# Weight loads on a second queue and reordered statistics in the opening of a layernorm, local attention and gated MLP kernel

## The chip, the cores and the metric

The kernel runs on one core of a Trainium2 chip. The metric is the device time in microseconds (us) of one execution; lower is better. A profile of one execution has a "span" (first to last instruction), which is about 1.8 us shorter than the time. Times inside a profile count from the start of the span.

The program is static: Python code plans every instruction with a model of durations, and writes one instruction list for each engine. In the traces below each engine takes its list in order and waits on semaphores (in the changed kernel VectorE sat idle for 0.85 us in front of an instruction whose own inputs were ready).

## The reference

`x` has 2048 rows (tokens) of 640 numbers, all bfloat16.

```python
xn = layernorm(x)                        # per row, no weights
q, k, v = xn @ wqkv                      # 640 -> 3*640, 32 heads of 20
# sliding attention: each token sees 8 keys, at distances 0, 2, ..., 14
o = softmax(q.k * 20**-0.5) . v
out = x + o @ wo + ((xn @ w_gate) * (xn @ w_up)) @ w_down
```

Only the opening matters here: x is cut into 16 tiles of 128 tokens; each tile is loaded, normalised, transposed, and then multiplied with the Q and K weights.

## The kernel before

How a tile goes through the opening (`op` plans one instruction on one engine, `Task` hands it to the planner; `dve` is VectorE, `act` ScalarE, `pe` TensorE, `sp` the sync engine, which here only issues DMAs):

```python
def front(t):
    # ... cut: names of the tile's buffers
    def stats(i):      # VectorE: statistics of one half of the 640 columns
        op("dve", lambda e: e.bn_stats(o, a), ...)
    def aggr():  ...   # VectorE: mean and variance from both halves
    def sqrt():  ...   # ScalarE: standard deviation
    def recip(): ...   # VectorE: 1 / standard deviation
    def apply(): ...   # VectorE for t < 6, one instruction of 640 columns

    yield have("x", t)
    if t == 1:
        yield have("sd", 0)              # tile 1 may start once tile 0's sqrt is planned
    for i in range(2):
        if t == 2 and i == 1:
            yield have("xnt", 1)
        yield Task("dve", lambda: stats(i), r=[x], prio=-1 if t == 1 and i == 0 else p)
    yield Task("dve", aggr, ...)
    yield Task("act", sqrt, ...)
    yield Task("dve", recip, ...)
    yield Task("dve" if t < N_DVE_A else "act", apply, ...)
    # ... cut: 5 transposes on TensorE into PSUM, then the copy back to SBUF
    #     (tile 0: columns 0-383 by VectorE, the rest by ScalarE); mark("xnt", t)
```

How the opening loads are issued, all but the touch on the sync queue:

```python
    x_load(0)
    stores.append(dma(TCH[0:16], tch, ..., name="touch", eng="act"))   # 5 KB of the weights, result unused
    x_load(1)
    wqkv_load(0, 0, 3)       # Q weights, first 3 of 5 chunks, 480 KB
    wqkv_load(0, 3, NCH)     # Q weights, last 2 chunks, 320 KB
    x_load(2)
    wqkv_load(1, 0, 3)       # K weights, the same way
    wqkv_load(1, 3, NCH)
    x_load(3)
    K.t["act"] = 2.1         # the planner takes ScalarE to be free from 2.1 us
    warm(18)                 # 18 matmuls of zeros, result unused
```

An x tile is 160 KB. After tile 0's transposes three more warm-up matmuls follow. The planner's belief about a load is one formula: it starts 1.2 us after its issue or when the load before it is through, moves 280 KB per us, and lands 0.8 us later.

Of the kernel before, what the change touches and what calls it, by code (L numbers as in the profile page):

```python
# [6 lines left out]
ALU = mybir.AluOpType  # L7
# [3 lines left out]
D = 640  # L11
NCH = 5
# [9 lines left out]
TS = 128  # L22
# [27 lines left out]
class Sched:  # L50
# [74 lines left out]
                deps[q.idx] = q  # L125
        return deps

    def op(self, eng, fn, r=(), w=(), dma=False, name="", occ=None, lat=None, lock=False, nbytes=0, mode=0, group=None, extra=0.0, acc=0.0):
        X = _Op()
        X.eng, X.fn, X.name, X.dma, X.group = eng, fn, name, dma, group  # L130
        X.needs_tick, X.event, X.pre_know, X.idx = False, None, None, len(self.ops)
        X.nth = self.n_eng[eng]
        self.n_eng[eng] += 1
        rk = [k for a in r for k in self.keys(a)]
        wk = [k for a in w for k in self.keys(a)]
        deps = self.deps_of(eng, rk, wk)
        if occ is None and not dma:
            occ = 0.1
        inorder = eng in ("pe", "act", "dve")
        start = max([self.t[eng]] + [d.end for d in deps.values()])  # L140
        if lock:
            start = max(start, self.t_lock)
        if eng == "pe" and mode != self.pe_mode:
            start += 0.1
            self.pe_mode = mode
        if dma:
            self.t[eng] = start + (0.48 if occ is None else occ)
            if acc:
                self.t_acc = max(self.t_acc, start + 3.8) + acc
                X.end = self.t_acc  # L150
            else:
                self.t_data = max(self.t_data, start + 1.2) + nbytes / 280e3
                X.end = self.t_data + 0.8 + extra
        else:
            self.t[eng] = start + occ
            X.end = start + (occ if lat is None else lat)
        if lock:
            self.t_lock = start + occ
        last = {}
        keep = []  # L160
        for d in deps.values():
            if d.dma or d.eng == "pool":
                keep.append(d)
            else:
                b = last.get(d.eng)
                if b is None or b.idx < d.idx:
                    last[d.eng] = d
        X.deps = keep + list(last.values())
        for d in X.deps:
            if not d.dma:  # L170
                d.needs_tick = True
        for k in rk:
            st = self.state.get(k)
            if st is None:
                self.state[k] = [None, [X]]
            elif inorder and st[1] and st[1][-1].eng == eng and not st[1][-1].dma:
                st[1][-1] = X
            else:
                st[1].append(X)
        for k in wk:  # L180
            self.state[k] = [X, []]
        if dma:
            if group is None or group not in self.groups:
                sem = self.nc.alloc_semaphore(f"dma{self.n_dma}")
                self.n_dma += 1
                if group is not None:
                    self.groups[group] = [sem, []]
            if group is None:
                X.event = (sem, 16)
            else:  # L190
                g = self.groups[group]
                g[1].append(X)
                X.event = (g[0], 16)
        self.ops.append(X)
        return X
# [151 lines left out]
def build_kernel(nc, A_x, A_wqkv, A_wo, B_x, B_w_gate, B_w_up, B_w_down, out):  # L347
    K = Sched(nc)
    op = K.op
# [3 lines left out]
    def sb(name, shape, dtype=BF16, at=None):  # L353
        n = mybir.dt.size(dtype)
        for s in shape[1:]:
            n *= s
        n = (n + 63) // 64 * 64
        if at is None:
            at = place[0]
            place[0] += n  # L360
        assert at + n <= 229344, (name, at + n)
        return K.sbuf(name, shape, dtype, at)
# [10 lines left out]
    NXS = 12  # L373
    XST = sb("XST", [128, NXS, D], at=a_ot + NCH * JB * 2)
# [43 lines left out]
    XNS = sb("XNS", [128, NXN, D], at=a_xr)  # L418
# [3 lines left out]
    MV = sb("MV", [128, NT, 2], FP32)  # L422
    SD = sb("SD", [128, NT, 4], FP32)
    DUM = sb("DUM", [128, 16], FP32)
    TCH = sb("TCH", [128, NCH, 32])
    ZERO = sb("ZERO", [128, JB])
    EPSC = sb("EPSC", [128, 16], FP32)
    IDENT = sb("IDENT", [128, 128])
# [15 lines left out]
    def mark(*k):  # L444
        done.add(k)
# [4 lines left out]
    def have(*k):  # L450
        return lambda: k in done
# [4 lines left out]
    xhbm = A_x[0]  # L456
    ohbm = out[0]

    def dma(o, i, r=(), w=(), name="", eng="sp", group=None):
        n = mybir.dt.size(o.dtype)  # L460
        for s in o.shape:
            n *= s
        return op(eng, lambda e: e.dma_start(o, i), r=r, w=w, dma=True, name=name, nbytes=n, group=group)  # L463

    op("dve", lambda e: e.memset(ZERO[:], 0.0), w=[ZERO[:]], name="zero", occ=0.2)
    op("dve", lambda e: e.memset(EPSC[:], EPS), w=[EPSC[:]], name="epsc", occ=0.1)
# [3 lines left out]
       r=[IDENT[:]], w=[IDENT[:]], name="ident", occ=0.4)  # L470
# [3 lines left out]
       r=[G[:]], w=[G[:]], name="g1", occ=0.3)  # L474
    op("pool", lambda e: e.affine_select(G[:], G[:], pattern=[[-4, H]], compare_op=ALU.is_ge,
                                         fill=0.0, base=0, channel_multiplier=1),
       r=[G[:]], w=[G[:]], name="g2", occ=0.3)
    op("pool", lambda e: e.memset(KT[:, :, 0:PAD], 0.0), w=[KT[:, :, 0:PAD]], name="kpad", occ=0.3)

    def xslot(t):  # L480
        return t + 4 if t < 8 else t - 8

    def x_load(t, eng="sp"):
        dma(XST[:, xslot(t), :], xhbm[t * TS:(t + 1) * TS, :], w=[XST[:, xslot(t), :]], name=f"xld{t}", eng=eng)
        mark("x", t)

    wqkv_src = A_wqkv.rearrange("(c p) n -> p c n", p=128)

    def wqkv_load(g, lo=0, hi=NCH):
        dst = WQKV[:, WPOS[g], lo:hi, :]  # L490
        dma(dst, wqkv_src[:, lo:hi, g * D:(g + 1) * D], w=[dst], name=f"ld_wqkv{g}_{lo}")

    def loads():
        def t(f, *a):
            return Task("sp", lambda: f(*a), prio=0)

        for t_ in range(4, NXS):
            yield t(x_load, t_)
        yield t(wqkv_load, 2)
        for t_ in range(NXS, NT):  # L500
            yield have("apply", t_ - NXS)
            yield t(x_load, t_)

        def w(T, src):
            dma(T[:], src.rearrange("(c p) n -> p c n", p=128), w=[T[:]], name="ld_w")

        def pads():
            z = ZERO[:, 0:PAD].unsqueeze(1).to_broadcast([128, NCH, PAD])
            dma(vscr[:, 0:PAD].rearrange("(c p) s -> p c s", p=128), z, r=[ZERO[:, 0:PAD]], w=[("vscr", "pad")], name="vpad")

        yield have("xnt", NT - 1)
        yield t(w, WG, B_w_gate)
        yield t(pads)
        yield t(w, WU, B_w_up)
# [15 lines left out]
    def front(t):  # L530
        x, st = XST[:, xslot(t), :], STATS[:, t, 0:12]
        xs, mv = XNS[:, t % NXN, :], MV[:, t, 0:2]
        sd, rstd, nmr = SD[:, t, 0:1], SD[:, t, 1:2], SD[:, t, 2:3]
        p = 0.1 * t

        def stats(i):
            o, a = st[:, 6 * i:6 * i + 6], x[:, i * DHALF:(i + 1) * DHALF]
            op("dve", lambda e: e.bn_stats(o, a), r=[a], w=[("st", t, i)], name=f"bn{t}_{i}", occ=0.49)  # L538
# [8 lines left out]

        def recip():
            op("dve", lambda e: e.reciprocal(rstd, sd), r=[("sd", t)], w=[("rstd", t)], name=f"rstd{t}", occ=0.16)  # L549
            if t >= N_DVE_A:  # L550
                op("dve", lambda e: e.tensor_scalar(nmr, mv[:, 0:1], rstd, -1.0, op0=ALU.mult, op1=ALU.mult),
                   r=[("mv", t), ("rstd", t)], w=[("nmr", t)], name=f"nmr{t}", occ=0.13)

        def apply():
            if t < N_DVE_A:
                op("dve", lambda e: e.tensor_scalar(xs, x, mv[:, 0:1], rstd, op0=ALU.subtract, op1=ALU.mult),
                   r=[x, ("mv", t), ("rstd", t)], w=[xs], name=f"lnap{t}", occ=0.45)
            else:
                op("act", lambda e: e.activation(xs, x, ACT.Identity, bias=nmr, scale=rstd),
                   r=[x, ("nmr", t), ("rstd", t)], w=[xs], name=f"lnap{t}", occ=0.75)  # L560
            mark("apply", t)
# [2 lines left out]
        if t == 1:  # L564
            yield have("sd", 0)
        for i in range(2):
            if t == 2 and i == 1:
                yield have("xnt", 1)
            yield Task("dve", lambda: stats(i), r=[x], prio=-1 if t == 1 and i == 0 else p)
        yield Task("dve", aggr, r=[("st", t, 1)], prio=p)  # L570
        yield Task("act", sqrt, r=[("mv", t)], prio=p - 1)
# [1 line left out]
        if t >= NXN:  # L573
            yield have("xnt", t - NXN)
        yield Task("dve" if t < N_DVE_A else "act", apply, r=[("rstd", t), x], w=[xs], prio=p)
        o = XNT[:, :, t * TS:(t + 1) * TS]
        if t < N_PE_T:
# [624 lines left out]
    stores = []  # L1202
# [65 lines left out]
    N_DVE_A = 6  # L1268
# [9 lines left out]
    H_PRIO = 9  # L1278
    FIN_PRIO = 8

    x_load(0)
    tch = A_wqkv.rearrange("(c k p) n -> k c p n", k=16, c=NCH)[:, :, 0, 0:32]
    stores.append(dma(TCH[0:16], tch, w=[TCH[0:16]], name="touch", eng="act"))
    x_load(1)
    wqkv_load(0, 0, 3)
    wqkv_load(0, 3, NCH)
    x_load(2)
    wqkv_load(1, 0, 3)
    wqkv_load(1, 3, NCH)
    x_load(3)  # L1290
    K.t["act"] = 2.1
    warm(18)

    def misc():
# [67 lines left out]
```

## Time and profile before

The time before was 270.0 us (median of 3, 269.71 to 270.01).

| | before | read from |
|---|---|---|
| span | 268.9 us | the page |
| TensorE (PE) busy | 262.7 us, 98% (18 of the 1783 matmul records are missing) | the page |
| first projection starts | 7.30 us | PE timeline |
| last gap before PE runs through | ends at 9.64 us | PE timeline |

The chain that ended last, from the page (shares of the span by engine, then by line):

```profile
span 268.9 us, 4464 instructions
...
PE 94%; DMA 2%; DVE 2%; issue 1%; SPq 0%; DVEq 0%
```

Nearly all is TensorE; the 2% of DMA is one load. The same chain in order of time (start, length, what), around that load:

```profile
1.73 5.44 DMA WQKV<-in_A_wqkv_dram
7.17 0.14 issue
7.30 0.84 PE PS L640 x12
...
9.09 0.50 DVE XNT L604
9.60 0.05 issue
9.64 1.98 PE PS L640 x32
```

The first projection (L640) hung on the first Q weight load, issued at 1.73 and landed at 7.17. The PE timeline (start, length, engine, line, operation; in brackets the idle time before it and what ended it):

```profile
1.27 4.02 PE L624 MATMUL PS<-ZERO 128*128 128x256 bf16 x18 [1.27 <-DVE EPSC L466]
5.42 0.71 PE L585 MATMUL PS<-IDENT,XNS 128*128 128x128 bf16 x5
5.92 0.85 PE L624 MATMUL PS<-ZERO 128*128 128x256 bf16 x3
7.30 1.48 PE L640 MATMUL PS<-XNT,WQKV 128*128 128x128 bf16 x20 [0.53 <-DMA WQKV<-in_A_wqkv_dram]
8.61 0.44 PE L585 MATMUL PS<-IDENT,XNS 128*128 128x128 bf16 x5
9.64 1.98 PE L640 MATMUL PS<-XNT,WQKV 128*128 128x128 bf16 x32 [0.59 <-DVE XNT L604]
```

L624 are warm-ups, L585 transposes. PE is nearly without a hole from 1.27 to 6.77. VectorE in the same stretch:

```profile
3.22 0.89 DVE L538 BATCH_NORM_STATS2 STATS<-XST 128x6 f32<-128x320 bf16 x2 [1.98 <-DMA XST<-in_A_x_dram]
4.14 0.21 DVE L541 BATCH_NORM_AGGREGATE MV<-STATS 128x2 f32<-128x12 f32 x1
4.27 0.44 DVE L538 BATCH_NORM_STATS2 STATS<-XST 128x6 f32<-128x320 bf16 x1
4.71 0.16 DVE L549 RECIPROCAL SD<-SD 128x1 f32<-128x1 f32 x1
4.91 0.45 DVE L556 TENSOR_SCALAR XNS<-XST,MV,SD 128x640 bf16<-128x640 bf16 x1
```

The third line is already tile 1: its first half of statistics fills the time in which VectorE would wait for tile 0's square root.

### The profile page before, as it was taken

To read this page: it belongs to the slowest core of one execution; us is meant where nothing else is said; L and a number is where in the kernel's file an instruction comes from. 1 tells how busy PE (TensorE), PEld (TensorE's weight loads), DVE (VectorE), ACT (ScalarE), POOL (GpSimd) and SP (SyncE) were. 2 spreads that over 40 slices of the span, in tenths; PEclk is the share of its full clock that TensorE was granted. 3 is DMA by queue.
4 is the path that set the end of the run, shared out by engine and by line. 5 is a ranking of instruction groups with operands and counts; after the bars stand their busy time and mean duration, and the time that the engine had idled before them with its cause. 6 is when DMAs were issued, how large, how long until landed. Compare 5 with 4: busy or idle time off the path is not lost.

```text
span 268.9 us, 4464 instructions
## 1 busy us (share of the span) xinstructions
PE 262.7 (98%) x1765; PEld 152.8 (57%) x1783; DVE 222.9 (83%) x282; ACT 105.4 (39%) x188; POOL 130.3 (48%) x81
## 2 busy tenths in 40 slices
PE   7899999999999999999999999999999999999996
PEld 5796975444444444444444445765457654676775
DVE  4678899999999997379999899999999989992212
ACT  3369998556723232245344353024430342201000
POOL 1000000000004439900199999999999879985000
PEclk9999999999999999999999999999999999999999
DMA  6954479621414998087025953465534561022201
GB/s 206 367 188 74 98 105 339 247 97 56 142 39 113 234 244 177 0 268 151 2 52 140 240 118 79 132 176 138 152 79 130 148 195 42 27 73 61 87 28 49
DMA packets 40261, 35.58 MB, mean 132 GB/s; under 512 B 15408, under 2 KB 38448, under 8 KB 40240
## 3 DMA queue, kind: packets, MB, share of 16 engines
q1 hardware_dynamic: 39424, 33.15, 45.4%
q0 software_dynamic: 576, 2.10, 3.9%
q8 instruction: 14, 0.23, 0.4%
q10 hardware_dynamic: 240, 0.05, 0.1%
q14 instruction: 7, 0.06, 0.1%
HBM read 25.07 MB, written 5.26 MB: 113 GB/s over the span
## 4 chain that ended last, share of the span: by engine, by line
PE 94%; DMA 2%; DVE 2%; issue 1%; SPq 0%; DVEq 0%
PE PS L1149 36%; PE PS L1231 28%; PE PS L640 24%; PE PS L903 3%; DMA WQKV<-in_A_wqkv_dram 2%; PE PS L1098 2%; DVE HT L1158 1%; PE PS L585 0%; DVE RS L952 0%; DVE LOG L956 0%; SPq L463 0%; DVE XNT L604 0%; DVE SM L932 0%; DVE FOUT L1244 0%; DVEq L325 0%
## 5 line engine op out<-in xcount | busy, mean ns | idle before, releaser
L1056 POOL TENSOR_TENSOR SV<-PV 128x1024 bf16<-128x1024 f32 x40 | 93.5, 2366 | 24.7 <-DVE LOG L956 18.7
L1051 DVE TENSOR_TENSOR PV<-VX,PS 128x1024 f32<-128x1024 bf16 (+1 forms) x56 | 91.8, 1670 | 0.3 <-POOL SV L1056 0.3
L640 PE MATMUL PS<-XNT,WQKV 128*128 128x512 bf16 (+2 forms) x474 | 66.4, 299 | 1.6 <-DVE XNT L604 0.6
L1149 PE MATMUL PS<-XNT,WU 128*128 128x512 bf16 x239 | 59.6, 380 | 0.2
L1149 PE MATMUL PS<-XNT,WG 128*128 128x512 bf16 x229 | 57.3, 380 | 0.7 <-issue 0.3
L640 PEld LDWEIGHTS PS<-XNT,WQKV 128*128 128x128 bf16 x480 | 43.6, 113 | 23.8 <-DVE SD L549 1.0
L1149 PEld LDWEIGHTS PS<-XNT,WU 128*128 128x128 bf16 x240 | 23.3, 98 | 28.7 <-ACT XNT L645 0.8
L1149 PEld LDWEIGHTS PS<-XNT,WG 128*128 128x128 bf16 x240 | 23.2, 98 | 28.6 <-issue 0.8
L792 DVE TENSOR_TENSOR PRD<-QT,KT 128x2048 bf16<-128x2048 bf16 x32 | 36.8, 1217 | 0.0
L1244 DVE TENSOR_TENSOR FOUT<-PS,XR 128x320 bf16<-128x320 f32 (+1 forms) x33 | 15.7, 479 | 22.2 <-PE PS L1231 22.0
L1231 PE MATMUL PS<-WD,HT 128*128 128x320 bf16 x192 | 28.7, 300 | 0.0
L645 ACT ACTIVATE HT<-PS 128x512 bf16<-128x512 f32 x24 | 14.3, 596 | 34.0 <-PE PS L1149 34.0
L1231 PE MATMUL PS<-WO,OT 128*128 128x320 bf16 (+1 forms) x165 | 27.0, 296 | 0.0
L863 POOL TENSOR_TENSOR PRF<-PRF,PRF 128x1024 f32<-128x1024 f32 x4 | 9.4, 2352 | 33.1 <-DVE PRF L837 33.0
L1107 ACT ACTIVATE OT<-PS 128x512 bf16<-128x512 f32 x20 | 10.5, 600 | 34.4 <-PE PS L1098 34.4
L922 POOL MEMSET LOG<- 32x6 bf16 (+6 forms) x7 | 0.4, 95 | 48.4 <-ACT LOG L914 48.4
L1158 DVE TENSOR_TENSOR HT<-HT,PS 128x512 bf16<-128x512 bf16 x24 | 16.3, 680 | 8.7 <-PE PS L1149 7.0
L1231 PEld LDWEIGHTS PS<-WD,HT 128*128 128x128 bf16 x192 | 18.8, 98 | 7.6
L1231 PEld LDWEIGHTS PS<-WO,OT 128*128 128x128 bf16 x165 | 15.7, 98 | 6.6 <-issue 0.8
L837 DVE TENSOR_TENSOR PRF<-PS,KT 128x1024 f32<-128x1024 f32 x16 | 19.0, 1216 | 0.4 <-DMA PRF<-PRF 0.4
L538 DVE BATCH_NORM_STATS2 STATS<-XST 128x6 f32<-128x320 bf16 x32 | 14.7, 471 | 3.0 <-DMA XST<-in_A_x_dram 3.0
L1231 PE MATMUL PS<-WD,XNT 128*128 128x320 bf16 (+1 forms) x108 | 14.6, 285 | 0.0
(58 smaller groups left out, 216.1 us busy)
## 6 DMA issues: line engine op xcount, KB each, us to landing
VX<-v_scratch SPq DMA_DIRECT2D x80, 130.0 KB, 2.9
XST<-in_A_x_dram SPq DMA_DIRECT2D x16, 160.0 KB, 6.2
v_scratch<-VST SPq DMA_DIRECT2D x4, 640.0 KB, 4.3
XR<-in_A_x_dram SPq DMA_DIRECT2D x16, 160.0 KB, 2.9
out_dram<-FOUT SPq DMA_DIRECT2D x15, 160.0 KB, 1.8
PRF<-PRF POOLq DMA_DIRECT2D x4, 512.0 KB, 8.6
WG<-in_B_w_gate_dram SPq DMA_DIRECT2D x1, 1920.0 KB, 8.6
WU<-in_B_w_up_dram SPq DMA_DIRECT2D x1, 1920.0 KB, 12.1
```

The lines of the kernel that those rows point to most:

```text
L538: op("dve", lambda e: e.bn_stats(o, a), r=[a], w=[("st", t, i)], name=f"bn{t}_{i}", occ=0.49)
L640: op("pe", (lambda o, l, x, c, first: lambda e: e.matmul(o, l, x, start=first, stop=(c == NCH - 1)))(o, l, x, c, first), r=[l, x], w=[o], ...
L645: X = op("act", (lambda o, i: lambda e: e.activation(o, i, ACT.Copy))(o, i), r=[i], w=[o], name=name, occ=0.12 + n * 0.9e-3)
L792: op("dve", lambda e: e.tensor_tensor(s[:], qb, kv, ALU.mult), r=[q, rk], w=[s[:]], name=f"prod{j}_{r}_{c}", occ=1.15, lock=True)
L837: X = op("dve", lambda e: e.tensor_tensor(o[:], qb, kv, ALU.mult), r=[q, rk], w=[o[:]], name=f"prow{j}_{r}_{c}_{q0}", occ=1.17)
L1051: op("dve", lambda e: e.tensor_tensor(p, vw, a, ALU.mult), r=[vv] + rk, w=[p], name=f"pv{u}_{x}_{r0}", occ=0.09 + 1.1 * nr)
L1056: X = op("pool", lambda e: e.tensor_tensor(o, p[:, :, 0, :], p[:, :, 1, :], ALU.add), r=[p[:]] + tokens(), w=[o], name=f"pva{u}_{x}", occ= ...
L1107: X = op("act", (lambda o, b: lambda e: e.activation(o, PS[:, b, :], ACT.Copy))(o, b), r=[PS[:, b, :]], w=[o], name=f"oev{u}", occ=0.58)
L1149: op("pe", (lambda l, x, c: lambda e: e.matmul(PS[:, b, :], l, x, start=(c == 0), stop=(c == NCH - 1)))(l, x, c), r=[l, x], w=[PS[:, b, :] ...
L1158: X = op("dve", lambda e: e.tensor_tensor(h, h, PS[:, hold[1], :], ALU.mult), r=[h, PS[:, hold[1], :]], w=[h], name=f"h{m}_{j}", occ=0.65)
L1231: op("pe", (lambda l, x, i: lambda e: e.matmul(dst, l, x, start=(i == 0), stop=(i == n - 1)))(l, x, i), r=[l, x], w=[PS[:, b, :]], name=f" ...
L1244: X = op("dve", lambda e: e.tensor_tensor(o, PS[:, b, 0:wid], xr, ALU.add), r=[PS[:, b, :], xr], w=[o], name=f"fin{t}_{nb}", occ=0.15 + wi ...
```

## The change

The intent: the weights should come sooner, so they are issued first thing on the scalar queue, which is idle, while the x tiles stay on the sync queue; x tile 3 waits until tile 0's reciprocal, so as not to compete. Tile 0 is applied in two parts, so that three transposes can start before the rest is applied. Half of tile 1's statistics and all of tile 2's go behind the copies that PE waits for. The planner is told a landing time for each load (`land=`) in place of its formula.

```diff
-    def op(self, ..., acc=0.0):
+    def op(self, ..., acc=0.0, land=None):
+            if land is not None:
+                X.end, self.t_data = land, max(land - 0.8, self.t_data - nbytes / 280e3)
     # x_load, wqkv_load and dma pass land and the queue on
     def x_load(t, ...):
+        r = [("rstd", 0)] if t == 3 else []          # x tile 3 after tile 0's reciprocal
     def apply():
-            if t < N_DVE_A:
+            if t == 0:
+                for a, b in ((0, 384), (384, D)):    # ... tensor_scalar of columns a to b
+            elif t < N_DVE_A:
     # in front(t):
-            if t == 2 and i == 1:
-                yield have("xnt", 1)
+            if t == 2 and i == 0:
+                yield have("apply", 1)
+            if t in (1, 2) and i == 1:
+                yield have("xnt", t - 1)
     # the opening loads:
-    x_load(0)
-    stores.append(dma(TCH[0:16], tch, w=[TCH[0:16]], name="touch", eng="act"))
-    x_load(1)
-    wqkv_load(0, 0, 3)
-    wqkv_load(0, 3, NCH)
-    x_load(2)
-    wqkv_load(1, 0, 3)
-    wqkv_load(1, 3, NCH)
-    x_load(3)
-    K.t["act"] = 2.1
+    x_load(0, land=3.2)
+    wqkv_load(0, 0, 3, "act", 5.4)
+    x_load(1, land=4.3)
+    wqkv_load(0, 3, NCH, "act", 6.7)
+    x_load(2, land=5.7)
+    wqkv_load(1, 0, 3, "act", 7.9)
+    wqkv_load(1, 3, NCH, "act", 8.9)
+    K.t["act"] = 4.1
     warm(18)
# ... cut: removal of the buffer TCH, argument lists, mark("rstd", t); loads() now starts
#     with x tile 3 and waits for tile 0's reciprocal
```

## The prediction

> **What bounds the kernel.** The chain of waits puts 94% of the 268.9 us span on the tensor engine (PE busy 98%, granted clock 1.00) and only 2% on a DMA: the Q weight load, issued at 1.73 us, ends 5.44 us later (7.17). The PE timeline shows the only real hole in its first 9.64 us: warm-up matmuls, five transposes (5.42), three more warm-ups (to 6.77), 0.5 us waiting for weights, 20 Q matmuls of tile 0 from 7.30 (1.48), transposes of tile 1 (8.61), then 0.59 idle until tile 1's copy ends. From 9.64 on PE runs almost gapless to 266. So up to 9.64 it has done only about 1.9 us of useful work: anything won can be won there alone, at most some 3 us.
>
> Why is the weight late? The DMA packets of the trace: one 1280-byte packet of that first weight load, started at 3.56, took 2.05 us; the other lanes had delivered by about 5.0. The following loads' completions inherit the roughly 2 us lag (x tile 2 lands at 8.47, the first K part at 9.8). The small touch load did not prevent it. Tile 1's chain adds its part: DVE waits for x tile 2 until 8.49, runs its first statistics there, and only then copies tile 1.
>
> **What the change does.** It removes the 5 KB touch, starts the Q and K weights at about 0.83, 1.25, 1.7, 2.1 on the scalar queue (0.43 us each) instead of 1.73, 2.2, 3.25, 3.7, and defers x tile 3 until tile 0's reciprocal (about 4.9). Bytes are unchanged. The Trainium skill, "DMA: Bandwidth & Descriptors", section "Issuing engines are not separate DMA queues", says that both queues use the same 16 engines and interleave, so only issue time is saved; I expect no more bandwidth, but the slow first weight packet about 1.4 us earlier. Costs: the 1.28 us activation table load moves to about 2.6 to 3.9, still before the first square root (4.38); x tiles 0 and 1 share the engines with weights, so they may land 0 to 0.5 us later (before: 3.2 and 3.6). Splitting tile 0's apply adds one DVE instruction (an estimate of 0.1 us from the 0.45 us whole) and lets three transposes start some 0.15 us earlier, but the 18 warm-ups end at 5.29 anyway. Moving half of tile 1's statistics (0.49 us) behind tile 0's copy frees DVE for that copy about 0.2 us earlier.
>
> **Expected times.** Q weights land near 5.4 and 6.7, K weights near 7.9 and 8.9. The first projection then hangs on tile 0's copy and the warm-ups: near 6.3 instead of 7.30. K matmuls of tile 0 fill the gap that waited for tile 1. The continuous stretch gains 1.0 + about 0.4 = 1.4 us, an estimate.
>
> **Does it survive?** From 9.64 to the end PE is the chain; DVE waits on that chain around 128 to 133 us cost PE nothing. GpSimd's last sum ends at 245.4 and PE takes it at 247.1: 1.6 us of slack, so 1.4 us passes even if that branch does not move. But the static order of all engines is computed again from new assumed times; that may shift the later order by about a microsecond either way.
>
> **Prediction: 268.6 us, range 267.4 to 269.9.** Faster by over 2%: 0.02; within 2%: 0.96; slower by over 2%: 0.02.
>
> **Right if** the first projection starts at 6.0 to 6.6, K matmuls precede tile 1's Q, the chain's DMA piece shrinks below 1%, and PE busy time is unchanged. **Wrong if** the slow packet also holds up x tile 0 (first statistics after 3.7), if a weight load still ends after 7, if the table load delays the first square root, or if the recomputed order starves PE later, after 100 us.

## The result, and the profile after

| | median | range | executions |
|---|---|---|---|
| before | 269.69 us | 269.48 to 270.01 | 6 |
| after | 271.55 us | 270.55 to 271.92 | 6 |

Ratio 1.0058, 95% interval 1.0038 to 1.0078: slower by 0.6%. Within 2%, so of the predicted class, but outside the predicted range and of the wrong sign. A ratio here is the mean time of one kernel's fast executions over that of the other's of the same rounds, so it is not quite the ratio of the medians. Executions in which one die ran at a lower clock are left out of the means. The spread, 1.37 us, is more than twice that of before, 0.53.

The page of after, the chain that ended last:

```profile
span 269.8 us, 4479 instructions
...
PE 97%; DMA 2%; DVE 0%; SPq 0%; issue 0%
```

Its opening in order of time:

```profile
1.28 4.14 DMA XST<-in_A_x_dram
5.42 0.02 issue
5.44 0.49 DVE STATS L541
...
6.03 0.39 DVE XNS L562
...
7.82 2.13 PE PS L651 x20
```

The load on the chain is now an *x tile*, not a weight. VectorE and PE (line numbers moved by the change: L541 statistics, L552 reciprocal, L562 apply in parts, L596 transposes, L635 warm-ups, L651 projections):

```profile
3.46 0.89 DVE L541 BATCH_NORM_STATS2 STATS<-XST 128x6 f32<-128x320 bf16 x2 [2.22 <-DMA XST<-in_A_x_dram]
4.38 0.21 DVE L544 BATCH_NORM_AGGREGATE MV<-STATS 128x2 f32<-128x12 f32 x1
5.44 0.49 DVE L541 BATCH_NORM_STATS2 STATS<-XST 128x6 f32<-128x320 bf16 x1 [0.85 <-DMA XST<-in_A_x_dram]
5.85 0.14 DVE L552 RECIPROCAL SD<-SD 128x1 f32<-128x1 f32 x1
6.03 0.64 DVE L562 TENSOR_SCALAR XNS<-XST,MV,SD 128x384 bf16<-128x384 bf16 x2
```

```profile
1.27 4.02 PE L635 MATMUL PS<-ZERO 128*128 128x256 bf16 x18 [1.27 <-DVE EPSC L467]
6.47 0.72 PE L596 MATMUL PS<-IDENT,XNS 128*128 128x128 bf16 x5 [1.18 <-DVE XNS L562]
6.97 0.85 PE L635 MATMUL PS<-ZERO 128*128 128x256 bf16 x3
7.61 2.34 PE L651 MATMUL PS<-XNT,WQKV 128*128 128x128 bf16 x20
9.75 0.74 PE L596 MATMUL PS<-IDENT,XNS 128*128 128x128 bf16 x5
10.28 2.68 PE L651 MATMUL PS<-XNT,WQKV 128*128 128x128 bf16 x40
```

Two things went wrong. First, VectorE waited 0.85 us for x tile 1, with tile 0's reciprocal standing behind that wait; its square root had ended at 4.9. Tile 0 was applied at 6.03 instead of 4.91, although its own data came only 0.24 us later. Second, the same 20 matmuls of the first projection took 2.34 us instead of 1.48. The groups of PE instructions from 7 to 10.2 us (count, then busy time and mean ns of one), before:

```profile
L640 PE MATMUL PS<-XNT,WQKV 128*128 128x128 bf16 x30 | 2.2, 221 | 1.1 <-DVE XNT L604 0.6 <-DMA WQKV<-in_A_wqkv_dram 0.5
```

and after:

```profile
L651 PE MATMUL PS<-XNT,WQKV 128*128 128x128 bf16 x20 | 2.3, 314 | 0.0
```

314 ns for 221: the tensor clock was not yet released. In the instruction records these matmuls start 107 ns apart after and 56 ns apart before. The trace's own clock record begins at full clock at 6.77 us before, at 10.43 us after. (The page's row of the clock is no help: it shows 9, the top tenth, in its first slice too, as the record begins only with the release.)

Where the rest of the time went is quickly said: nowhere. On the chain in order of time the first sums of the logits start at 47.91 before and 48.85 after, and the last instruction at 266.56 and 267.50: the same 0.94 us at both. The loss is complete before 48 us, and almost all of it arises before 11.

The landings (last of a load's 16 completions, read from the trace; "believed" is what the planner of the changed kernel was told):

```
                 x0     x1     x2     Q first  Q rest  K first  K rest   (us)
before          3.20   3.61   8.46    7.17     8.03    9.80    10.71
after           3.44   5.42   6.96    4.97     6.39    8.09     8.99
believed        3.2    4.3    5.7     5.4      6.7     7.9      8.9
```

The weights did what was wanted of them. x tile 1, issued at 1.28 us in both kernels, paid: 1.8 us later. The packets of the trace show how it was served:

```
after: KB moved in quarter microseconds, by queue
from     2.50 2.75 3.00 3.25 3.50 3.75 4.00 4.25 4.50 4.75
sync       23   19    6    0    0    0   25   78   49    9
scalar      8   41   79   89   92   86   66   20   46   82
```

What the sync queue moved up to 3.25 us was x tile 0. The first packet of x tile 1 started at 4.04 us, when some 400 KB of the 480 KB weight load, issued 0.45 us before it, had been started. By 4.5 us the two queues were moving side by side again.

### The profile page after: what moved, and what is told of

The parts are those of the page before. It is cut to its first block, busy times and chain, and to the rows that moved or that the text cites. A ratio compares the mean times of both kernels' runs of the same rounds, so it can differ in the third digit from the quotient of the medians.

```text
span 269.8 us, 4479 instructions
## 1 busy us (share of the span) xinstructions
PE 265.0 (98%) x1783; PEld 154.2 (57%) x1783; DVE 223.1 (83%) x283; ACT 105.5 (39%) x188; POOL 130.3 (48%) x81
## 4 chain that ended last, share of the span: by engine, by line
PE 97%; DMA 2%; DVE 0%; SPq 0%; issue 0%
PE PS L1160 39%; PE PS L1242 28%; PE PS L651 25%; PE PS L914 3%; PE PS L1109 2%; DMA XST<-in_A_x_dram 2%; PE PS L596 1%; PE PS L635 0%; DVE STATS L541 0%; SPq L464 0%; DVE XNS L562 0%; DVE FOUT L1255 0%; DVE SD L552 0%
## 5 line engine op out<-in xcount | busy, mean ns | idle before, releaser
L651 PE MATMUL PS<-XNT,WQKV 128*128 128x512 bf16 (+2 forms) x480 | 68.0, 303 | 0.0
L1160 PE MATMUL PS<-XNT,WG 128*128 128x512 bf16 x240 | 59.7, 379 | 0.0
L651 PEld LDWEIGHTS PS<-XNT,WQKV 128*128 128x128 bf16 x480 | 44.8, 115 | 22.2 <-ACT LOG L925 0.8
L541 DVE BATCH_NORM_STATS2 STATS<-XST 128x6 f32<-128x320 bf16 x32 | 14.8, 473 | 3.1 <-DMA XST<-in_A_x_dram 3.1
```

The costliest lines, as they stand in the source:

```text
L541: op("dve", lambda e: e.bn_stats(o, a), r=[a], w=[("st", t, i)], name=f"bn{t}_{i}", occ=0.49)
L651: op("pe", (lambda o, l, x, c, first: lambda e: e.matmul(o, l, x, start=first, stop=(c == NCH - 1)))(o, l, x, c, first), r=[l, x], w=[o], ...
L1160: op("pe", (lambda l, x, c: lambda e: e.matmul(PS[:, b, :], l, x, start=(c == 0), stop=(c == NCH - 1)))(l, x, c), r=[l, x], w=[PS[:, b, :] ...
```

## The experiments

Three theories and their rival:

- **Theory 1**: x tile 1 is served behind the first Q weight load, and its statistics stand in front of tile 0's reciprocal on VectorE.
- **Theory 2**: the hole of 1.18 us in PE's warm-up moves the release of the clock to a later moment. (Every clock record that runs from the release to the end lasts a whole number of steps of 3.413 us: 259.41, 262.83 and 266.24 us are 76, 77 and 78 of them. Such a step is the "window" of the expectations.)
- **Theory 3**: the slow weight load in the first profile of before is not typical, so the baseline had less to win than was counted.
- **Rival**: the recomputed order, the split apply or the deferred x tile costs the time, later or by itself.

Four kernels went to a chip together; each was timed against the kernel before there. Where "program order unchanged" is said, the instruction lists of PE, VectorE and GpSimd were compared with those of the kernel it was made from, and differ in nothing but what the edit names.

### The changed kernel again

No edit.

> The changed kernel, unaltered, for a second look at what varies. Theory 1 (x tile 1 is served behind the whole first Q weight load, and its statistics stand in front of tile 0's reciprocal on VectorE): x tile 1 lands again near 5.4 us (5.2 to 5.6), reciprocal of tile 0 near 5.85. Theory 2 (the tensor clock is released one window later because PE idles from 5.3 to 6.5): release after 9 us in most executions, and the spread of the times, 270.5 to 272.0, is that release falling earlier or later. Rival (the late schedule is worse): the first 11 us look like those of before, and the loss appears after 20 us. Time 271.5, spread 1 us or more.

Five fast executions: 270.62, 270.72, 270.75, 271.65, 271.75; median of the fast ones 270.75, ratio 1.004 (1.0024 to 1.0056). The profiled one: clock 0.85, so its times prove little, but x tile 1 landed at 5.39 in it, as expected. Its clock record begins at 4.86 us, before PE's hole: the release can come early in the unaltered changed kernel, too. Together with the first six executions there are two groups and nothing between them: five with a span of 268.7 to 268.8 us, six with 269.7 to 270.1. Whether the clock was released after 9 us in most executions could not be checked here for want of a fast trace.

### Tile 0's applies in front of tile 1's statistics

```diff
         if t == 1:
-            yield have("sd", 0)
+            yield have("apply", 0)
```

This moves one VectorE instruction behind three others; PE's program order is unchanged.

> One VectorE instruction moved: the first half of tile 1's statistics goes behind tile 0's two applies. Theory 1: the wait for x tile 1 leaves tile 0's chain; reciprocal of tile 0 near 5.0 (was 5.85), transposes start near 5.55 (was 6.47), first projection 6.6 to 6.9 (was 7.61); that alone is worth about 0.8 us. Theory 2: PE's hole shrinks from 1.2 to about 0.3 us, the clock is released near 7, another 1.2 us. Both: 269.3 to 270.0. Theory 1 alone: 270.7. Rival (late schedule): 271.5, unchanged.

Measured: 269.95 us (269.89 to 269.99, 5 executions), before 269.96; ratio 0.9997 (0.9986 to 1.0009). VectorE and PE:

```profile
5.05 0.17 DVE L552 RECIPROCAL SD<-SD 128x1 f32<-128x1 f32 x1 [0.36 <-ACT SD L547]
5.26 0.64 DVE L562 TENSOR_SCALAR XNS<-XST,MV,SD 128x384 bf16<-128x384 bf16 x2
5.81 0.49 DVE L541 BATCH_NORM_STATS2 STATS<-XST 128x6 f32<-128x320 bf16 x1
```

```profile
5.69 0.71 PE L596 MATMUL PS<-IDENT,XNS 128*128 128x128 bf16 x5 [0.41 <-DVE XNS L562]
6.20 0.56 PE L635 MATMUL PS<-ZERO 128*128 128x256 bf16 x3
6.65 1.31 PE L651 MATMUL PS<-XNT,WQKV 128*128 128x128 bf16 x20
```

x tile 1 landed at 5.68, as late as in the changed kernel, but no longer held anything up. The first projection started 0.96 us earlier, the clock was released at 6.33, and the spread of 1.4 us shrank to 0.1. One instruction's place explains the whole loss. It also shows that the loss is not in the later order, which this kernel shares with the changed one. But the repaired change is *level* with before, not 1.4 us faster: this asked for theory 3.

### More warm-up matmuls

```diff
-    warm(18)
+    warm(24)
```

PE's and VectorE's order is otherwise unchanged; ScalarE copies two of the Q and K results out of PSUM in the other order.

> Six more warm-up matmuls (24 for 18), so that PE is busy until about 6.6 instead of 5.3; the wait for x tile 1 stays. Theory 2: the clock is released near 7 instead of 10.4, the 20 Q matmuls of tile 0 take about 1.2 us instead of 2.1, time 270.2 to 270.6 although the first projection still starts at 7.4 to 7.7. Theory 1 alone: no gain, 271.5. Rival (late schedule): 271.5.

Measured: 270.73 us (270.56 to 270.89), ratio 1.0026 (1.0014 to 1.0038), spans 268.7 to 268.9 in all five executions: the fast group of the changed kernel without the slow one. VectorE still waits for x tile 1, and PE still waits for VectorE, but it counts at full clock when it goes on:

```profile
6.76 0.54 PE L596 MATMUL PS<-IDENT,XNS 128*128 128x128 bf16 x5 [1.16 <-DVE XNS L562]
...
7.55 1.31 PE L651 MATMUL PS<-XNT,WQKV 128*128 128x128 bf16 x20
```

The clock was released at 4.45 us in this trace, so the later warm-ups ran at full clock and ended near 5.6, and PE's wait is as long as in the changed kernel, but harmless to the clock. In an execution with a later release, 24 warm-ups at the half-clock spacing of 0.213 us would last until 1.27 + 24 x 0.213 = 6.4 us (an estimate from the spacing in the changed kernel's trace), which closes the hole. This one trace would have released as early with 18 warm-ups; what counts is that none of the five executions is in the slow group, where 6 of 11 were. (Alone, that could be chance about 6 times in 100; the next experiment is the other half of the test.) So the two costs come apart: theory 2 is the distance between the groups, some 1.1 us in about half of the executions; theory 1's wait is what is left between this kernel and the repaired one, 268.7 against 268.0 us of span.

### Fewer warm-up matmuls

```diff
-    warm(18)
+    warm(12)
```

The dose in the other direction; nothing else moves.

> The changed kernel with 12 warm-up matmuls for 18: PE falls idle near 4.0 instead of 5.3, so its hole before the transposes grows from 1.2 to about 2.5 us; nothing else moves. Theory 2 (the hole decides at which window the tensor clock is released): no window that ends between about 5 and 9 is busy enough, so nearly every execution is a late one: release after 9 in the trace, times 271.4 to 272 with few or none near 270.6; median 271.6. If the hole does not decide: same two groups as the changed kernel, about half and half.

Measured: 272.23 us (271.55 to 272.55, 6 executions), ratio 1.0074 (1.0056 to 1.0091). No execution was in the fast group.

```profile
6.58 0.71 PE L596 MATMUL PS<-IDENT,XNS 128*128 128x128 bf16 x5 [2.57 <-DVE XNS L562]
7.09 0.85 PE L635 MATMUL PS<-ZERO 128*128 128x256 bf16 x3
7.73 2.34 PE L651 MATMUL PS<-XNT,WQKV 128*128 128x128 bf16 x20
```

The clock was released at 12.09 us in the trace. The median was 0.6 us worse than expected, as the release can come even later than in the changed kernel's trace. With 12, 18 and 24 warm-ups 6 of 6, 6 of 11 and 0 of 5 executions had a span of 269.7 us or more. With 18 warm-ups and a hole of only 0.41 or 0.43 us (the two repaired kernels) it was 0 of 11. So PE's hole decides.

The Trainium skill, "TensorE: Matmul & The Clock Gate", section "What's actually happening", says why: a monitor watches free-running windows of about 3.4 us, and the clock goes from half to full after a busy one. The traces agree with the half and full rates (107 and 56 ns between starts). They agree with the window too: the clock records are multiples of 3.413 us, and they begin anywhere from 4.45 to 12.09 us.

How much idle time a window may hold can be bracketed from the traces. Count PE's idle time (transposes are work here) in the 3.413 us before each release, and in the steps before that. Released: 0.43 us idle (the fitted change), 0.41 (tile 0's applies first), 0.13 (before). Not released, with the warm-ups already running: 0.68 (x tile 1 in front of the weights), 1.18 (the changed kernel), 1.25 and 1.32 (12 warm-ups). So here the limit lies between 0.43 and 0.68 us. From that follows an estimate for the changed kernel, whose warm-ups run from 1.27 to 5.29 us: a window whose end falls anywhere between 4.68 less the limit and 5.29 plus the limit releases early. That is 1.5 to 2.0 us out of 3.4, about half of all starts, and 5 of 11 executions did. With 12 warm-ups, which last 2.7 us, at least 0.67 us of any window is idle: 0 of 6 did.

### x tile 1 issued in front of the weights

```diff
+    x_load(1, "act", land=4.3)
     wqkv_load(0, 0, 3, "act", 5.4)
-    x_load(1, land=4.3)
```

Program order of PE, VectorE and GpSimd unchanged.

> x tile 1 is issued on the scalar queue in front of the first Q weight load; the other three weight loads follow as before; program order of PE, VectorE and GpSimd untouched. Theory 1: x tile 1 lands at 3.5 to 3.9, the first Q weight near 5.4, x tile 2 still about 7; reciprocal of tile 0 near 5.0; first projection near 6.4. Time 269 to 269.8 if the clock follows (theory 2), 270.5 if it does not. If engines shared their time evenly between queues, x tile 1 would have landed early in the changed kernel too, and this would change its landing by less than 0.5 us.

Measured: 271.54 us (270.23 to 272.13), ratio 1.005 (1.0031 to 1.0069): a miss. x tile 1 landed at 4.00, 0.1 us past the expected range, and VectorE's reciprocal no longer waited for it (5.33). But x tile 0, now sharing the DMA engines with tile 1, landed at 3.82; the first Q weight landed at 7.22 in this trace and the rest of Q at 8.88, with a packet of 1.5 us among the weights'; PE had a hole of 0.68 us before the transposes, and the clock was released at 10.17. One tile's lateness had been exchanged for others. Two things are worth keeping. The service is not strictly one load after the other: x tiles 0 and 1, issued within 0.01 us on the two queues, moved side by side (48 and 45 KB in the quarter from 2.75), and x tile 2 moved beside the weight load that was issued 0.02 us before it. And a weight load can be slow in a two-queue kernel too.

### The kernel before again

No edit.

> The kernel before, unaltered, for a second trace: its first profile spanned 268.9 us, while its timed executions span 268.0 to 268.4. Theory 3 (the 2 us packet of the first Q weight load that I read in the first profile is not in a typical execution, so the baseline has less to win than I counted): this trace shows no packet over 1 us in the first 6 us, the first Q weight lands at 5.0 to 5.4 instead of 7.17, the first projection starts at 6.2 to 6.6 instead of 7.30, span near 268.2. Rival: the slow packet is there in every execution and the span differs for another reason.

Measured: 269.99 us (269.65 to 270.40), spans 267.9 to 268.7. The chain of the second profile of before in order of time:

```profile
1.73 4.50 DMA WQKV<-in_A_wqkv_dram
...
6.36 0.84 PE PS L640 x12
...
8.71 1.98 PE PS L640 x32
```

No packet took over 0.85 us; the first Q weight landed at 6.23 instead of 7.17 (expected: 5.0 to 5.4, too early), and everything after it is 0.93 us earlier than in the first profile. From the last gap on, both profiles take the same time to the last instruction: 266.56 - 9.64 = 256.92 and 265.62 - 8.71 = 256.91 us. So the first profile of before showed an execution about a microsecond worse than this one in just the stretch that the change was to improve. The wait for the weight in the second profile:

```profile
6.36 1.48 PE L640 MATMUL PS<-XNT,WQKV 128*128 128x128 bf16 x20 [0.22 <-DMA WQKV<-in_A_wqkv_dram]
```

Neither profile is the middle. The 33 executions of before span 267.6 to 269.0 us, with a median of 268.3, and only one reaches 268.9. The first profile is thus about 0.6 us worse than the median, the second 0.4 better. The slow weight load is no freak, though: the last experiment below shows one again. Theory 3 holds, with some 0.6 us of the expected gain as its size.

### The queue alone

In the kernel before, only the queue of four loads is exchanged and the touch removed; the planner still believes in one queue, so that the order of PE, VectorE and GpSimd stays exactly that of before.

```diff
-        return op(eng, ..., dma=True, name=name, ...)
+        X = op(eng, ..., dma=True, name=name, ...)
+        X.eng = "act" if name[:8] in ("ld_wqkv0", "ld_wqkv1") else X.eng; return X
-    stores.append(dma(TCH[0:16], tch, ..., name="touch", eng="act"))
```

> The kernel before with one part of the change: the touch is gone and the four Q and K weight loads are issued on the scalar queue; x tile 3 undeferred, program order of PE, VectorE and GpSimd exactly that of before. Theory 1: x tile 1 lands near 5.4 (before 3.6), tile 0's reciprocal waits for it (5.85 instead of 4.7), first projection after 7.2. Theory 2: the clock is released at about 10 in some of the executions. Time 270.5 to 271.7, spread 1 us or more: the loss of the whole change comes from this part. Rival (the new program order or the split costs it): 269.5 to 270.0.

Measured: 270.85 us (270.59 to 272.44), ratio 1.0046 (1.0025 to 1.0067). x tile 1 landed at 5.40:

```profile
5.42 0.49 DVE L538 BATCH_NORM_STATS2 STATS<-XST 128x6 f32<-128x320 bf16 x1 [0.65 <-DMA XST<-in_A_x_dram]
5.84 0.14 DVE L549 RECIPROCAL SD<-SD 128x1 f32<-128x1 f32 x1
```

The instruction that was harmless at 4.27 in the kernel before now holds tile 0 up. This part of the change, on the old order, gives the loss by itself, spread included. The trace has no clock record, but PE's matmuls start 107 ns apart until 9.59 us and 56 ns apart from 9.68, so the release was late here too.

This trace also limits what may be said of the DMA queues. Early on it repeats the changed kernel: no packet of x tile 1 until 4.0 us. But from 7.0 to 9.25 us, with x tiles 3 and on not held back, the sync queue moved 40 to 46 KB and the scalar queue 42 to 49 KB in every quarter microsecond. The last K weights, issued at 2.39 us, landed at 11.00, after three x tiles issued 0.3 to 1.4 us later on the other queue (9.43, 10.46, 10.84). So "first issued, first served" is not a rule here, and what held x tile 1 back is not known.

### Everything but the queue

The changed kernel, with the four loads back on the sync queue, in the order of before, and its own program order kept.

```diff
-        return op(eng, ..., land=land)
+        X = op(eng, ..., land=land)
+        X.eng = "sp" if name[:8] in ("ld_wqkv0", "ld_wqkv1") else X.eng; return X
+    x_load(1, land=4.3)
     wqkv_load(0, 0, 3, "act", 5.4)
-    x_load(1, land=4.3)
```

> The other part alone: the changed kernel with its program order, its split apply and its deferred x tile 3, but the four weight loads go out on the sync queue in the order of before (x tiles 0 and 1 first). Theory 1: x tile 1 lands at 3.6, tile 0's reciprocal near 4.8, first projection 6.1 to 6.5 unless a slow weight packet hits; PE idle under 0.3 us before the transposes, clock released before 8.7 in every execution, spread under 0.5 us. Time 269.3 to 270.0, level with before or a little better. Rival (the new program order or the split costs the microsecond): 271 or more.

Measured: 270.71 us (270.10 to 272.48), ratio 1.0036 (1.0011 to 1.0061): worse than expected. x tile 1 landed at 3.63 and the first projection started at 6.32, both as expected. The profiled execution is the fastest of the six (span 268.4 us, like before's), so it does not show the loss itself. What it does show is a wait a moment later:

```profile
9.08 2.43 PE L651 MATMUL PS<-XNT,WQKV 128*128 128x128 bf16 x40 [0.79 <-DMA WQKV<-in_A_wqkv_dram]
```

The planner believed that the K weights land at 7.9, and so put tile 0's K in front of tile 1's Q. On one queue they land at 9.03, and PE waits. It is theory 1's pattern on another engine: a list ordered by a landing that does not come. Whether this costs the slower executions their time is asked by the next run.

### Everything but the queue, with the landings of that trace

```diff
-    x_load(0, land=3.2)
-    x_load(1, land=4.3)
-    wqkv_load(0, 0, 3, "act", 5.4)      # ... and so on
+    x_load(0, land=3.1)
+    x_load(1, land=3.6)
+    wqkv_load(0, 0, 3, "act", 5.8)      # then 6.7, x tile 2 7.1, K 9.1 and 10.0
```

> The one-queue run again with the landings of its own trace given to the scheduler (K weights 9.1 and 10.0 instead of 7.9 and 8.9). PE then takes tile 1's Q before tile 0's K. If the 0.6 us that the one-queue run lost on before is PE waiting for K weights that the program expects too early (0.79 us in its trace): 269.6 to 270.1, spread under 0.6. If it is the split apply or the reordered statistics: 270.5 to 271 again.

Measured: 269.94 us (269.78 to 270.44), before 270.23, ratio 0.9996 (0.998 to 1.0013). The wait for K weights is gone, and so are the slow executions (spans up to 268.7 us, not 270.7). How one wait could make some of those so slow was not traced. So the split apply, the reordered statistics and the deferred x tile 3 cost nothing that can be seen here, and win nothing; this was the rival's last place.

### The changed kernel with the landings of its own trace

```diff
-    x_load(0, land=3.2)
-    wqkv_load(0, 0, 3, "act", 5.4)
-    x_load(1, land=4.3)                 # ... and so on
+    x_load(0, land=3.5)
+    wqkv_load(0, 0, 3, "act", 5.0)
+    x_load(1, land=5.4)                 # then Q 6.4, x tile 2 7.0, K 8.1 and 9.0
```

> The changed kernel with the landings measured in its own trace given to the scheduler (x tile 0 3.5, x tile 1 5.4, x tile 2 7.0, Q weights 5.0 and 6.4, K weights 8.1 and 9.0) in place of the assumed ones. The scheduler then writes by itself the VectorE program of the run that moved one instruction. Theory 1: 269.8 to 270.1, spread under 0.4 us, clock released before 8.7. If that earlier gain was chance: 271.

Measured: 269.93 us (269.77 to 270.22, 6 executions), ratio 0.9994 (0.998 to 1.0008), spans 267.9 to 268.2, clock released at 5.73. The planner wrote the VectorE list of the second experiment without being asked (on ScalarE two copies out of PSUM change places). This is the change as it was meant: level with before, its interval including no gain at all, with a narrower spread.

### Without the touch

```diff
-    stores.append(dma(TCH[0:16], tch, ..., name="touch", eng="act"))
```

> The kernel before without the 5 KB touch, nothing else. If the touch spares the weight load a slow first access: 0.5 to 2 us slower, and a first Q weight landing after 6. If it does nothing, as the slow packet in the first profile suggests: 269.7 to 270.2, same landings as before. In theory 1 the touch plays no part.

Measured: 269.85 us (269.66 to 270.39), ratio 0.9999 (0.9981 to 1.0016), the first Q weight at 5.79. Removing the touch costs nothing that can be seen.

### Tile 1's copy in front of tile 2's statistics

Two VectorE instructions of the kernel before exchanged, nothing else.

```diff
+    # after planning: move the first half of tile 2's statistics behind tile 1's copy
+    Y = K.ops.pop(index of "bn2_0"); K.ops.insert(index of "xntcp1" + 1, Y)
     K.emit(stores)
```

> The kernel before with two VectorE instructions exchanged and nothing else: the first half of tile 2's statistics, which waits for x tile 2 (8.5 in the first trace, 7.5 in the second), goes behind tile 1's copy. The copy then follows the transposes of tile 1: PE's idle stretch before tile 1's Q (0.59 us in both traces) shrinks to about 0.35. Expected 269.7, that is 0.2 to 0.3 us faster than before; this is what the sound part of the change is worth by itself. No change at all: the wait for x tile 2 is not on the chain.

Measured: 270.32 us (269.58 to 270.89), ratio 1.0004 (0.9987 to 1.0021): no gain, and the idle stretch before tile 1's Q did not shrink:

```profile
8.66 0.44 PE L585 MATMUL PS<-IDENT,XNS 128*128 128x128 bf16 x5
9.69 1.48 PE L640 MATMUL PS<-XNT,WQKV 128*128 128x128 bf16 x23 [0.58 <-DVE XNT L604]
```

The copy takes 0.49 us and needs the transposes to be through. In the two profiles of before they were at 9.07 and 8.14 us, and the statistics had ended at 8.98 and 8.06. The wait for x tile 2 that I had read as part of tile 1's chain was hidden. This trace, by the way, has the slow weight load again: the first Q weight landed at 7.20, and the profiled span is 269.2.

### What the landings say together

| trace | x0 | x1 | first Q weight | first projection | span |
|---|---|---|---|---|---|
| before, first profile | 3.20 | 3.61 | 7.17 | 7.30 | 268.9 |
| before, second profile | 3.14 | 3.63 | 6.23 | 6.36 | 267.9 |
| before, two statistics swapped | 3.10 | 3.59 | 7.20 | 7.33 | 269.2 |
| change on one queue, fitted | 3.17 | 3.55 | 5.90 | 6.41 | 268.2 |
| change | 3.44 | 5.42 | 4.97 | 7.61 | 269.8 |
| change, fitted | 3.57 | 5.36 | 4.91 | 6.64 | 268.0 |

In the six traces of one-queue kernels the first Q weight landed at 5.8 to 7.2 us; in the seven in which it came right behind x tile 0 on the other queue, at 4.9 to 5.3. So the change does bring the weight earlier, by 0.5 to 2.3 us. But with the weight out of the way the first projection hangs on tile 0's own chain, and that starts 0.2 to 0.7 us later, as x tile 0 lands at 3.4 to 3.7 instead of 3.0 to 3.2 (the reciprocal at 5.09 in the fitted change, at 4.66 in the second profile of before). That is where the rest of the expected gain went.

## Why the prediction was wrong, point by point

- *"The hole is the weight"*: the mechanism was right for the one execution that was profiled; the size was not. "0.5 us waiting for weights" with the first projection at 7.30 was an execution near the slow end. In the second profile it started at 6.36 after a wait of 0.22 us. The estimated gain of "1.0 us" from 7.30 to 6.3 was measured against a start that was nearly there already; against the median execution of before, about 0.6 us of it did not exist. The warning was in the numbers: the profiled execution took 270.63 us and the three timed ones 269.71 to 270.01.
- *"x tiles 0 and 1 ... may land 0 to 0.5 us later"*: this is the step that turned the sign. x tile 0 was 0.24 us later, x tile 1 1.81 us. I took from the skill's section that the queues "interleave" and shared the lateness out evenly. From 3.25 to 4.0 us they did not interleave.
- *What stands behind x tile 1*: the prediction asks whether the slow packet holds up x tile 0, and never what tile 1's landing releases. Both the profile (the statistics line at 4.27 between aggregate and reciprocal) and the diff (an untouched line) showed that tile 0's reciprocal stood behind it. Its cost in span, from the kernel with 24 warm-ups to the repaired one: 268.7 - 268.0 = 0.7 us.
- *The clock*: "granted clock 1.00" was quoted as a fact about the whole span. The warm-ups were counted only as something that occupies PE until 5.29, not as what keeps the clock coming. A hole of 1.18 us in them cost about 1.1 us in 6 of 11 executions, 0.6 us in the mean.
- *The sum*: 0.7 + 0.6 us lie over the repaired kernel, and that is level with before. In spans, the changed kernel's 11 fast executions average 269.3 us, the fitted one's 268.1; the difference of 1.3 (before rounding) is the sum of these two terms.
- *"Q weights land near 5.4 and 6.7, K weights near 7.9 and 8.9"*: right, to 0.5 us (4.97, 6.39, 8.09, 8.99). *The table load stays in front of the first square root*: right (3.10 to 4.38, square root at 4.62). *Tile 0's K fills PE ahead of tile 1's Q*: right; the wait for K weights in the kernel with everything but the queue shows that order.
- *"The static order is computed again; that may shift the later order by about a microsecond"*: it did not. The 0.94 us lost by 48 us are the 0.94 us lost at the end.
- *Tile 1's copy waits behind tile 2's statistics*: wrong; exchanging the two changed nothing.
- *The other marks of "right if"*: the chain's DMA piece was 1.5% of the span, not under 1%. PE busy time reads 265.0 us after and 262.7 before, but with 18 records missing before, this mark cannot be judged.

What stays open: why x tile 1's packets waited for most of a weight load, while x tiles 0 and 1, issued together, shared, and so did K weights and x tiles in the run with the queue alone; why a weight packet sometimes takes 1 to 2 us; and a fast trace of an unaltered changed kernel with an early release was not caught, so that the fast group is identified by its span and by the warm-up runs.

## What to carry to other kernels

In a statically ordered program a load's landing time is an input to the *order* of every engine: when loads are moved to another queue, ask for each landing that gets later what stands behind it in the list of the engine that waits, and put the measured landings back into the planner. Before costing a gain of a microsecond, check that the profiled execution is a typical one: compare its time with the timed ones, and take a second profile. A hole in the warm-up matmuls can be paid twice, once as idle time and once as half clock for the work behind it: here 1.18 us of hole, and another 1.1 us in 6 of 11 executions.

## What the Trainium skill lacked or had wrong

- "DMA: Bandwidth & Descriptors", sections "Issuing engines are not separate DMA queues" and "Queues, rings and completion order", say that DMAs from different queues interleave, and that each DMA engine takes turns between queues packet by packet. In the changed kernel no packet of the 160 KB load moved for 0.75 us while a 480 KB load issued 0.45 us earlier on the other queue ran; it landed at 5.42 instead of 3.61 us. Elsewhere the traces agree with the page: loads issued within 0.02 us of one another shared (48 and 45 KB in a quarter of a microsecond), and so did K weights and x tiles from 7.0 to 9.25 us in the run with the queue alone. The turns are among queues that have work; whether x tile 1's packets already stood in their queue at 3.25 us, no trace here shows.
- The same page's rule, in "Rules for kernel authors", that spreading loads over issuing engines "only saves sequencer issue time" leaves out a cost: in all seven two-queue traces with the Q weights right behind x tile 0, x tile 1 landed at 5.4 to 5.7 us, for 3.5 to 3.6 with one queue.
- "TensorE: Matmul & The Clock Gate", section "HAM oscillation — how this bites in real kernels", warns of idle gaps over about 3.4 us. That is for a clock already released; for the first release the page asks for a busy window, but gives no figure for the idle time that a window may hold. Here windows with 0.43 us or less released it, and windows with 0.68 us or more did not; a gap of 1.18 us moved the release to 10.43 us in one trace, and one of 2.57 us to 12.09.
- "DMA: Bandwidth & Descriptors", section "Latency and other measured facts", gives 0.2 us for an HBM access and 2 us at high load, but does not say that one packet alone can be slow and hold up its whole load. Here one weight packet of 1280 bytes took 2.05 us where most took 0.055, and the next landings came late with it (7.17, 8.03 and 8.46 us, against 6.23, 7.09 and 7.54 in the second profile). Of the six one-queue traces two have the first Q weight past 7 us, one at 6.23, and three before 6.
